# Pairing lone output tiles across sequences, and spreading a row by transposition

## The chip, the cores and the metric

The kernel runs on one core of a Trainium2 chip. The metric is the device time of one execution in microseconds (us), and the time before is the median of three runs. A profile of one execution goes with it. Engines are named as in the profile: PE is TensorE (PEld its weight loads), DVE is VectorE, ACT is ScalarE, POOL is GpSimd, SP is SyncE, which here issues almost all DMA.

## The reference

Attention with RMS-normalised q and k over 8 sequences, 12 heads, 448 tokens and head size 64 is followed by an RMS norm over the 768 features and a gated feed-forward block without bias (768 to 1536 to 768), all in float32. Shortened:

```python
def rmsnorm(x, g):
    return x / np.sqrt(np.mean(x * x, axis=-1, keepdims=True) + 1e-06) * g

q_n, k_n = rmsnorm(q, g_q), rmsnorm(k, g_k)          # (8, 12, 448, 64)
attn = softmax(q_n @ k_n.T / 8)
x = (attn @ v).transpose(0, 2, 1, 3).reshape(3584, 768)

xn = rmsnorm(x, rms_g)
g = xn @ w_gate                                      # (3584, 1536)
out = (g * sigmoid(g) * (xn @ w_val)) @ w_out        # (3584, 768)
```

## The kernel before

All eight sequences are worked off in one program. The attention of sequence b+1 is interleaved on TensorE with the feed-forward work of the sequences before it: a list of items is handed out between the attention steps in proportion to what the items cost. Items are the output products of sequence b-1 and then the gate and value products of sequence b. After the last sequence's attention the rest of the list runs alone.

**Strassen's scheme (Winograd's form).** From sequence 1 on, the gate and value products, and the output products, take 7 block products where a plain matrix product of 2x2 blocks takes 8. For the output product the left matrix is h (1536 features, kept with the features in partitions), its two block rows are two tiles of 128 tokens, "a pair", and its block columns are features 0 to 767 and 768 to 1535. The right matrix is w_out, cut into B11, B12, B21, B22 of 768 x 384 and the derived T1 to T4. Sequence 0 multiplies plainly with the unchanged blocks, since the derived ones are made only after all weights have been converted.

**Tiles of tokens.** 448 tokens are three and a half tiles. An even sequence leaves its last 64 tokens to the odd one after it, which then has 512, four tiles:

```python
for fc in (fp, fp + NFP):                            # NFP = 6: chunk of 128 features
    st["h", b, fc] = free_h.pop(0)
    if b % 2:
        before = st.pop(("h", b - 1, fc))
        nc.gpsimd.tensor_copy(st["h", b, fc][:, 0:64], before[:, S - 64:S])
        free_h.append(before)
```

So an odd sequence has two pairs; an even one from 2 on has one pair and a tile alone ("s"), which takes the four original blocks:

```python
def out_order(b):
    if b % 2:
        return [(name, (0, 1)) for name in ORDER_O]
    order = [(name, (0, "s") if name[0] == "B" else (0,)) for name in ORDER_O]
    return order[:-1] + [("B12", ("s",))] + order[-1:]

ORDER_O = ("B11", "B21", "T2", "T3", "T1", "B22", "T4")
```

The sums of the left blocks are made by VectorE in the same chunk's gate and value step (`quad`), four instructions of 128 x 128 for a pair and chunk:

```python
for pair in range(1 + b % 2) if b >= FIRST_O else ():            # FIRST_O = 1
    if fp == 0:
        st["so", b, pair] = {name: raw_pool.tile([128, NFP, 128], F32, name="so", tag="raw")
                             for name in ("S1", "S2", "S4")}
    of = lambda name: left_o(b, pair, name, fp)
    nc.vector.tensor_tensor(of("S1"), of("A21"), of("A22"), ALU.add)
    ...                                                          # cut: S2, S3, S4 alike
```

The products themselves: six matmuls for one name and one pair, in two halves of three. B21 adds onto the PSUM bank of B11, and B22 onto that of T1:

```python
def step(name, which, half, last):
    onto = {"B21": "B11", "B22": "T1"}.get(name)
    ...                                                          # cut: the bank of "s"
    first = onto is None
    if half == 0:
        bank[name, which] = fresh() if first else bank[onto, which]
    for c in range(3 * half, 3 * half + 3):
        ...                                                      # cut: a is the left block
        nc.tensor.matmul(ps, lhsT=a, rhs=data(("wo", b, name, c)), start=first and c == 0, ...)   # L1086
    ...
# done(name, pair), after the second half:
#   B11: ScalarE copies the bank to p1            B21: ScalarE copies the bank out as y
#   T2:  VectorE  u2 = bank + p1                  T3:  VectorE  u3 = bank + u2
#   T1:  VectorE  y = bank + u3                   B22: VectorE  y = bank + u2
#   T4:  VectorE  y = bank + u3
```

Sequence 0 multiplies each tile plainly, 12 matmuls for each half of 384 output columns (`project_out`, L983), for `tiles = 3 + b % 2` = 3 tiles.

**Weights.** They are converted once, in 72 pieces that go through load, ScalarE, VectorE and a GpSimd add (`convert`, one piece at a turn), and written to a scratch tensor in DRAM. After that a weight block of 128 x 384 is loaded anew for each use into one of a set of buffers. When the conversion is over, its own buffers join them:

```python
if turn_of["n"] == TURNS:
    free_w.extend(cv_pool.tile([128, BW], F32, name="top") for _ in range(4))   # 25 + 4
```

The derived blocks of sequence 1 and on (T1 to T4) are made by VectorE while sequence 1 is worked on, and written to the scratch tensor too.

**The row of the norm.** The factor of each token is made with tokens in partitions (rs, 112 x 4) and is needed as a row over tokens, the same in all 128 partitions. A matmul with the identity does it, rs being read with step 0 as a 112 x 128 weight:

```python
for t in range(NT):                                              # NT = 4, P = 112
    nc.tensor.matmul(ps[:, t * P:(t + 1) * P], lhsT=rs[:, t:t + 1].to_broadcast([P, 128]),
                     rhs=ident[0:P, 0:P], start=True, stop=True)                 # L649
```

VectorE then multiplies x by that row out of PSUM.

Of the kernel before, what the change touches and what calls it, by code (L numbers as in the profile page):

```python
# [20 lines left out]
NT, P = 4, 112  # L21
# [314 lines left out]
def safe_scores(  # L336
# [306 lines left out]
    def norm_x(b):  # L643
# [4 lines left out]
        for t in range(NT):  # L648
            nc.tensor.matmul(ps[:, t * P:(t + 1) * P], lhsT=rs[:, t:t + 1].to_broadcast([P, 128]), rhs=ident[0:P, 0:P],  # L649
                             start=True, stop=True)  # L650
# [101 lines left out]
    turn_of = {"n": 0}  # L752
    TURNS = len(pieces) + 7
# [9 lines left out]
    def convert():  # L763
# [18 lines left out]
        if turn_of["n"] == TURNS:  # L782

            free_w.extend(cv_pool.tile([128, BW], F32, name="top") for _ in range(4))
# [3 lines left out]
    def out_order(b):  # L788


        if b % 2:
            return [(name, (0, 1)) for name in ORDER_O]
        order = [(name, (0, "s") if name[0] == "B" else (0,)) for name in ORDER_O]
        return order[:-1] + [("B12", ("s",))] + order[-1:]
# [4 lines left out]
    for b in range(1, B):  # L799
# [4 lines left out]
        if b < FIRST_O:  # L804
            uses += [("wo", b, *block_of(n, fc)) for n in range(2) for fc in range(NFC)]
        else:
            uses += [("wo", b, name, c) for name, _ in out_order(b) for c in range(NFP)]
# [85 lines left out]
    def quad(b, fp):  # L893
# [33 lines left out]
        def p2():  # L927
            product(b, fp, "A12", "B21", onto=bank["a"])
            for fc in (fp, fp + NFP):
                st["h", b, fc] = free_h.pop(0)  # L930
                if b % 2:

                    before = st.pop(("h", b - 1, fc))
                    nc.gpsimd.tensor_copy(st["h", b, fc][:, 0:64], before[:, S - 64:S])
                    free_h.append(before)
# [21 lines left out]
        def sums():  # L957

            for pair in range(1 + b % 2) if b >= FIRST_O else ():
                if fp == 0:  # L960
                    st["so", b, pair] = {name: raw_pool.tile([128, NFP, 128], F32, name="so", tag="raw") for name in ("S1", "S2", "S4")}
# [14 lines left out]
    def project_out(b, n, i, part, last):  # L976
# [5 lines left out]
        for fc in range(part * each, (part + 1) * each):  # L982
# [4 lines left out]
            if last and n == 1 and b % 2:  # L987
                free_h.append(st.pop(("h", b, fc)))
# [23 lines left out]
    def left_o(b, pair, name, c):  # L1012
# [4 lines left out]
        i = 2 * pair + row - 1  # L1017
        return st["h", b, c + (col - 1) * NFP][:, i * 128:(i + 1) * 128]
# [3 lines left out]
    def out_strassen(b):  # L1022
# [27 lines left out]
        def done(name, pair):  # L1050
# [4 lines left out]
            elif name == "B21":  # L1055
                final(ps, pair, 0, 2 * pair)
# [4 lines left out]
            elif name == "T1":  # L1061
                final(ps, pair, 1, 2 * pair + 1, "u3")
            elif name == "B22":
                final(ps, pair, 1, 2 * pair, "u2")
            else:
                final(ps, pair, 0, 2 * pair + 1, "u3")

        def step(name, which, half, last):
            onto = {"B21": "B11", "B22": "T1"}.get(name)
            if which == "s":  # L1070
                first = name in ("B11", "B22")
                if first and half == 0:
                    bank["s"] = fresh()
                ps = bank["s"]
            else:
                first = onto is None
                if half == 0:
                    bank[name, which] = fresh() if first else bank[onto, which]
                ps = bank[name, which]
            for c in range(3 * half, 3 * half + 3):  # L1080
                if which == "s":
                    fc = c + (int(name[1]) - 1) * NFP
                    a = st["h", b, fc][:, 256:384]
                else:
                    a = left_o(b, which, LEFT_O[name], c)
                nc.tensor.matmul(ps, lhsT=a, rhs=data(("wo", b, name, c)), start=first and c == 0, stop=c == NFP - 1,  # L1086
# [4 lines left out]
                if last and b % 2 and name in ("T3", "T4"):  # L1091
                    free_h.append(st.pop(("h", b, c + (name == "T4") * NFP)))
            if half == 0:
                return
            if which != "s":
                done(name, which)
            elif not first:
                final(ps, which, int(name[2]) - 1, 2)

        for name, whose in out_order(b):  # L1100
            for which in whose:
# [286 lines left out]
```

## Time and profile before

| what | before |
|---|---|
| time, median of 3 runs (lowest to highest) | 1614.12 us (1612.43 to 1615.44) |
| span of the profiled execution | 1612.2 us |
| HBM read, written | 235.93 MB, 39.32 MB |
| output matmuls of pairs and lone tiles (L1086), program | 534 |
| plain output matmuls of sequence 0 (L983), program | 72 |
| row-spreading matmuls (L649), program | 32 |
| loads of output weights (w<-kept_o), as listed | 289, 192.0 KB each, 3.0 us to landing |

A page of the profile has six parts: the busy time of each engine; the span in 40 slices with a digit for the tenths that an engine was busy in each; the DMA queues; the chain of work that ended last, followed back from the last instruction, by engine and by line; the costliest groups of instructions (line, engine, operation, output<-inputs, shapes, count | busy us, mean ns of one | idle time of the engine just before, and what ended it); and the DMA issues. The trace can also be asked for the groups with shapes kept apart, for who waited for whom, for a timeline, for the chain in order of time, and for the busy time of the engines within given stretches. Ends of matmuls are modelled, and a matmul's listed duration overlaps that of the next. Idle time of an engine that isn't the bottleneck costs nothing.

### The profile page before, as it was taken

To read this page: it belongs to the slowest core of one execution; us is meant where nothing else is said; L and a number is where in the kernel's file an instruction comes from. 1 tells how busy PE (TensorE), PEld (TensorE's weight loads), DVE (VectorE), ACT (ScalarE), POOL (GpSimd) and SP (SyncE) were. 2 spreads that over 40 slices of the span, in tenths; PEclk is the share of its full clock that TensorE was granted. 3 is DMA by queue.
4 is the path that set the end of the run, shared out by engine and by line. 5 is a ranking of instruction groups with operands and counts; after the bars stand their busy time and mean duration, and the time that the engine had idled before them with its cause. 6 is when DMAs were issued, how large, how long until landed. Compare 5 with 4: busy or idle time off the path is not lost.

```text
span 1612.2 us, 21593 instructions
## 1 busy us (share of the span) xinstructions
PE 1584.4 (98%) x7342; PEld 1123.7 (70%) x7342; DVE 859.9 (53%) x1495; ACT 472.3 (29%) x944; POOL 645.8 (40%) x667
## 2 busy tenths in 40 slices
PE   8999999999999999999999999999999999999998
PEld 4344445678865788568875788658786588959974
DVE  5989899278852455426562354524565235433531
ACT  6746564223221232223222222322332122101010
POOL 6867877434432354225533443344343223100000
PEclk9999999999999999999999999999999999999999
DMA  7648574567765555565544755476454454567651
GB/s 205 207 137 255 171 240 137 166 216 240 236 209 162 159 163 150 176 202 160 158 126 132 206 157 153 118 225 193 131 163 135 143 172 119 152 188 233 174 151 49
DMA packets 264586, 276.81 MB, mean 172 GB/s; under 512 B 79124, under 2 KB 261396, under 8 KB 264468
## 3 DMA queue, kind: packets, MB, share of 16 engines
q1 hardware_dynamic: 263540, 275.15, 57.3%
q8 instruction: 60, 0.98, 0.2%
q14 instruction: 58, 0.48, 0.1%
q10 hardware_dynamic: 800, 0.20, 0.1%
q0 software_dynamic: 128, 0.00, 0.0%
HBM read 235.93 MB, written 39.32 MB: 171 GB/s over the span
## 4 chain that ended last, share of the span: by engine, by line
PE 83%; DVE 4%; issue 0%; ACT 0%; DMA 0%; POOL 0%; DVEq 0%
PE ff L888 41%; PE ff L1086 22%; PE sc L537 6%; PE av L589 5%; PE ff L983 3%; PE sc L567 2%; PE den L602 2%; PE tr L519 1%; DVE top L736 1%; DVE top L737 1%; DVE rd L610 1%; PE ff L1117 0%; DVE top L735 0%; PE rb L649 0%; PE msx L637 0%
## 5 line engine op out<-in xcount | busy, mean ns | idle before, releaser
L888 PE MATMUL ff<-x,w 128*128 128x224 f32 x1740 | 354.2, 353 | 1.4 <-DVE u L900 1.4
L888 PEld LDWEIGHTS ff<-x,w 128*128 128x128 f32 x1740 | 326.5, 190 | 11.6 <-issue 4.6
L547 POOL TENSOR_TENSOR es<-e 128x448 f32<-128x448 f32 x82 | 91.3, 1134 | 528.6 <-ACT e L541 528.6
L888 PE MATMUL ff<-xs,w 128*128 128x224 f32 x1314 | 269.7, 353 | 5.4 <-DVE w L845 4.0
L888 PEld LDWEIGHTS ff<-xs,w 128*128 128x128 f32 x1314 | 246.1, 190 | 11.5 <-issue 9.9
L1086 PE MATMUL ff<-w,h 128*128 128x384 f32 x582 | 198.3, 487 | 0.0
L554 POOL TENSOR_TENSOR es<-es,e 64x448 f32<-64x448 f32 (+1 forms) x164 | 190.8, 1174 | 6.3
L610 DVE RECIPROCAL rd<-rd 128x448 f32<-128x448 f32 x41 | 121.0, 2952 | 124.8 <-ACT rd L609 124.8
L541 ACT ACTIVATE e<-sc,rs 128x448 f32<-128x448 f32 x288 | 161.9, 635 | 49.6 <-PE sc L537 46.7
L1086 PEld LDWEIGHTS ff<-w,h 128*128 128x128 f32 x582 | 109.1, 190 | 75.1 <-issue 2.0
L537 PE MATMUL sc<-qT,kT 64*128 64x448 f32 x576 | 139.1, 575 | 3.5 <-ACT sq L478 2.0
L589 PE MATMUL av<-e,vt 128*64 128x448 f32 x576 | 118.8, 548 | 0.0
L1086 PE MATMUL ff<-w,so 128*128 128x384 f32 x338 | 116.1, 488 | 1.3 <-DVE y L1047 1.3
L498 POOL TENSOR_TENSOR rs<-ms,mhalf 128x12 f32<-128x12 f32 (+1 forms) x50 | 114.5, 2290 | 4.2
L537 PEld LDWEIGHTS sc<-qT,kT 64*128 64x128 f32 x576 | 54.7, 186 | 85.6 <-issue 69.2
L1117 PE MATMUL ff<-x,w 128*128 128x448 f32 x288 | 111.8, 541 | 0.0
L900 DVE TENSOR_TENSOR cc<-ff,u 128x448 f32<-128x448 f32 x84 | 52.4, 623 | 90.4 <-PE ff L888 90.2
L1086 PEld LDWEIGHTS ff<-w,so 128*128 128x128 f32 x338 | 63.1, 190 | 45.6 <-DVE y L1047 2.5
L773 POOL TENSOR_TENSOR w<-top,raw 128x384 int32<-128x384 int32 x72 | 77.5, 1090 | 38.0 <-DVE top L737 25.4
L589 PEld LDWEIGHTS av<-e,vt 128*64 128x64 f32 x576 | 37.1, 136 | 75.6 <-issue 75.6
L1117 PEld LDWEIGHTS ff<-x,w 128*128 128x128 f32 x288 | 53.3, 190 | 50.8 <-issue 49.0
L623 POOL TENSOR_TENSOR ss<-ss,rd 128x448 f32<-128x448 f32 x40 | 46.6, 1165 | 79.3 <-ACT rd L622 79.3
(125 smaller groups left out, 1900.2 us busy)
## 6 DMA issues: line engine op xcount, KB each, us to landing
w<-kept SPq DMA_DIRECT2D x475, 192.0 KB, 2.8
w<-kept_o SPq DMA_DIRECT2D x289, 192.0 KB, 3.0
kept<-w SPq DMA_DIRECT2D x91, 192.0 KB, 3.9
top<-kept SPq DMA_DIRECT2D x77, 192.0 KB, 3.6
qk<-in_q_dram SPq DMA_DIRECT2D x48, 192.0 KB, 3.1
qk<-in_k_dram SPq DMA_DIRECT2D x96, 96.0 KB, 3.6
vt<-in_v_dram SPq DMA_DIRECT2D x48, 192.0 KB, 2.5
raw<-in_moe_w_gate_dram SPq DMA_DIRECT2D x24, 384.0 KB, 4.5
```

The source lines that it names most:

```text
L498: nc.gpsimd.tensor_tensor(st["rs", g][:, cols], ms, mhalf[:, cols], ALU.pow)
L537: nc.tensor.matmul(ps[:, 0:S], lhsT=kT[r, c * 128:(c + 1) * 128], rhs=qT[r, :], start=True, stop=True)
L541: nc.scalar.activation(e, ps[:, 0:S], ACT.Exp, scale=rs[:, n:n + 1])
L547: nc.gpsimd.tensor_tensor(es, st["e", g, 0, j], st["e", g, 1, j], ALU.add)
L554: nc.gpsimd.tensor_tensor(es[r], es[r], e[r], ALU.add)
L589: nc.tensor.matmul(av[own(j), 0:S], lhsT=vt[:, j, c], rhs=st["e", g, c, j], start=False, stop=(c == NK - 1), skip_group_check=True)
L610: nc.vector.reciprocal(rd, rd)
L773: nc.gpsimd.tensor_tensor(data(key).bitcast(I32), top, lo, ALU.add)
L888: nc.tensor.matmul(bank[:, w * HT:(w + 1) * HT], lhsT=wt[:, c * 128:(c + 1) * 128], rhs=x[:, c, :], start=onto is None and w == c == 0, st ...
L900: nc.vector.tensor_tensor(add[name], ps[:, 0:S], add[other], ALU.add)
L1086: nc.tensor.matmul(ps, lhsT=a, rhs=data(("wo", b, name, c)), start=first and c == 0, stop=c == NFP - 1, skip_group_check=True)
L1117: nc.tensor.matmul(bank[w][:, 0:S], lhsT=data(key)[:, c * 128:(c + 1) * 128], rhs=st["x", 0, half][:, c, :], start=half == c == 0, stop=ha ...
```

## The change

It has two parts.

The tiles of four sequences are now arranged together. A tile without a partner is not multiplied alone; its columns of h are copied by GpSimd into 12 "carried" tiles (128 x 128 each, index -1 below) and become the first tile of the next sequence's first pair. Sequence 0 multiplies two tiles plainly and carries its third, sequence 1 has four tiles and the carried one and carries its last, sequence 2 has three and the carried one, and sequence 3 takes sequence 2's last 64 tokens and has four; then it begins anew, with one pair in sequence 4. It is meant to save matmuls, as a tile in a pair takes fewer of them.

Room is made for it: the carried tiles and the sums S1, S2, S4 live in the former buffers of the conversion, so two buffers instead of four join the weight buffers. The blocks of h of a sequence that carries are given back later, after the copies.

The second part makes the row of the norm by TensorE's transposition instead of a matmul with the identity. The values are the same.

```diff
@@ norm_x
-            nc.tensor.matmul(ps[:, t * P:(t + 1) * P], lhsT=rs[:, t:t + 1].to_broadcast([P, 128]), rhs=ident[0:P, 0:P],
-                             start=True, stop=True)
+            nc.tensor.transpose(ps[:, t * P:(t + 1) * P], rs[:, t:t + 1].to_broadcast([P, 128]), ident[0:P, 0:P])
@@ convert
-            free_w.extend(cv_pool.tile([128, BW], F32, name="top") for _ in range(4))
+            free_w.extend(cv_pool.tile([128, BW], F32, name="top") for _ in range(2))
+            whole = [raw_pool.tile([128, 2 * BW], F32, name="raw") for _ in range(7)]
+            room_so.extend(whole[:6])
+            homes = [whole[6][:, 0:BW], whole[6][:, BW:]] + [cv_pool.tile([128, BW], F32, name="top") for _ in range(2)]
+            carried.extend(t[:, i * 128:(i + 1) * 128] for t in homes for i in range(3))
@@ in place of out_order
+    def out_pairs(b):
+        return (((0, 1),), ((-1, 0), (1, 2)), ((-1, 0), (1, 2)), ((0, 1), (2, 3)))[b % 4]
+
+    def carries(b):
+        return b % 4 < 2
@@ quad, p2
-                if b % 2:
+                if ("h", b - 1, fc) in st:
                     before = st.pop(("h", b - 1, fc))
-                    nc.gpsimd.tensor_copy(st["h", b, fc][:, 0:64], before[:, S - 64:S])
+                    if b % 2:
+                        nc.gpsimd.tensor_copy(st["h", b, fc][:, 0:64], before[:, S - 64:S])
+                    if carries(b - 1):
+                        at = out_pairs(b - 1)[-1][1] + 1
+                        nc.gpsimd.tensor_copy(carried[fc], before[:, at * 128:(at + 1) * 128])
                     free_h.append(before)
@@ quad, sums
-            for pair in range(1 + b % 2) if b >= FIRST_O else ():
+            for pair in range(len(out_pairs(b))):
                 if fp == 0:
-                    st["so", b, pair] = {name: raw_pool.tile([128, NFP, 128], F32, name="so", tag="raw") for name in ("S1", "S2", "S4")}
+                    st["so", b, pair] = {name: room_so[3 * pair + i].rearrange("p (c n) -> p c n", c=NFP)
+                                         for i, name in enumerate(("S1", "S2", "S4"))}
@@ left_o
-        i = 2 * pair + row - 1
-        return st["h", b, c + (col - 1) * NFP][:, i * 128:(i + 1) * 128]
+        i, fc = out_pairs(b)[pair][row - 1], c + (col - 1) * NFP
+        return carried[fc] if i < 0 else st["h", b, fc][:, i * 128:(i + 1) * 128]
@@ step: the branches for "s" go; the order is now
-        for name, whose in out_order(b):
-            for which in whose:
+        pairs = out_pairs(b)
+        for name in ORDER_O:
+            for which in range(len(pairs)):
                 for half in range(2):
@@ out_items, sequence 0
-        tiles = 3 + b % 2
+        tiles = out_pairs(b)[-1][1] + 1
```

Cut: the list of weight uses, which follows the same order, and the places where blocks of h are given back.

## The prediction

> **What bounds the kernel now.** I read the page first: the share of each engine, then the 40 slices, then the chain that ended last. The kernel runs on one core.
>
> ```profile
> span 1612.2 us, 21593 instructions
> PE 1584.4 (98%) x7342; PEld 1123.7 (70%) x7342; DVE 859.9 (53%) x1495; ACT 472.3 (29%) x944; POOL 645.8 (40%) x667
> PE   8999999999999999999999999999999999999998
> ...
> PEclk9999999999999999999999999999999999999999
> ...
> PE 83%; DVE 4%; issue 0%; ACT 0%; DMA 0%; POOL 0%; DVEq 0%
> PE ff L888 41%; PE ff L1086 22%; PE sc L537 6%; PE av L589 5%; PE ff L983 3%; PE sc L567 2%; PE den L602 2%; PE tr L519 1%; DVE top L736 1%; DVE top L737 1%; DVE rd L610 1%; PE ff L1117 0%; DVE top L735 0%; PE rb L649 0%; PE msx L637 0%
> ```
>
> TensorE (PE) is busy 98% of the span at full clock in every slice, and it holds 83% of the chain. All that is idle on it is 1612.2 - 1584.4 = 27.8 us. So the change is worth, first of all, what it takes off TensorE, and after that what it does to those few waits. L888 (gate and value products) is not touched; L1086 (paired output products), L983 (plain output products of sequence 0) and L649 (the row spread) are.
>
> Next I took the groups of TensorE with shapes kept apart, for how many records one matmul leaves, and the timeline for what one really takes. The durations in a group overlap one another (a matmul's end includes its drain), so I take the distance between starts.
>
> ```profile
> L1086 PE MATMUL ff<-w,h 128*128 128x384 f32 x582 | 198.3, 487 | 0.0
> ...
> L983 PE MATMUL ff<-w,h 128*128 128x384 f32 x144 | 47.7, 488 | 0.0
> ...
> L519 PE MATMUL tr<-ident,qn 128*128 128x128 f32 x144 | 24.0, 275 | 1.6 <-POOL qn L503 1.4 <-DMA kept<-w 0.2
> ...
> L649 PE MATMUL rb<-ident,rs 112*128 112x112 f32 x64 | 8.4, 275 | 1.0 <-POOL rs L641 1.0
> ```
>
> Counting the program: L983 issues 3 tiles x 2 halves x 12 = 72 matmuls and leaves 144 records; L649 issues 8 x 4 = 32 and leaves 64. A float32 matmul leaves two records. L519's transposes of q are 48 x 3 = 144 and leave 144: a transpose leaves one.
>
> ```profile
> 439.61 0.49 PE L519 MATMUL tr<-ident,qn 128*128 128x128 f32 x3
> 439.94 0.27 PE L523 MATMUL tr<-ident,rest 128*128 128x128 f32 x1
> ...
> 450.21 1.04 PE L649 MATMUL rb<-ident,rs 112*128 112x112 f32 x8
> 451.09 2.12 PE L1086 MATMUL ff<-w,h 128*128 128x384 f32 x6
> ```
>
> Columns: start, length, engine, line. Three transposes of 128 columns take 439.94 - 439.61 = 0.33 us, 0.11 us each. The four spreading matmuls take 451.09 - 450.21 = 0.88 us, 0.22 us each. For an output matmul I take the chain of waits in order of time, whose last long piece is the output of the last sequence, without attention between:
>
> ```profile
> 1551.41 54.19 PE ff L1086 x168
> ```
>
> 168 records are 84 matmuls: 54.19 / 84 = 0.645 us each.
>
> Last, who waited for whom on TensorE:
>
> ```profile
> PE ff L888 <- DVE w L845: 4.0, 2, 2.5
> PE ff L888 <- DVE u L900: 2.8, 2, 1.4
> PE ff L1086 <- DVE y L1047: 2.0, 3, 0.7
> ```
>
> The first two all lie between 316 and 448 us: the gate and value products of sequence 1, whose weight differences are made by VectorE (DVE) while it is also the busiest there (102 of 132 us). The third is the product of an unpaired even sequence: B22 adds onto T1's PSUM bank, and with one pair TensorE comes to it at once and has to wait until VectorE has read T1. Three even sequences (2, 4, 6), three waits.
>
> **What the Trainium skill says.** "Perfetto Trace Analysis", section Transposes, asks that logical transposes use the transpose operation and not a standard matmul, since it has a path that skips arithmetic. The trace agrees: one record in place of two, 0.11 us against 0.22 us. The same page, section Tensor Engine Instruction, says that a matmul's end in the profile is an estimate; here starts are 0.645 us apart for two records that are listed at 487 ns each, which is why I use starts. Its section Matmuls wants accumulation groups to rotate through banks so that evacuation overlaps; the three L1086 waits of 0.65 us are where that rotation is missing. "SBUF — State Buffer", in its summary rules, says that a VectorE instruction with two SBUF inputs contends with a GpSimd instruction that reads SBUF; the added copies and sums are of these kinds. No wait in the lists names it, so I give it only a place in the range.
>
> **The change part by part.**
>
> 1. Fewer output matmuls. A tile alone costs 24 (12 contraction chunks x 2 halves); a pair costs 7 products x 6 = 42, so 21 a tile. 3584 tokens are 28 tiles. Before: sequence 0 has 3 plain tiles, sequences 2, 4, 6 have one alone each, the other 22 make 11 pairs: 6 x 24 + 11 x 42 = 606. After: sequence 0 keeps 2 plain tiles (its weights are then still blocks of the original matrix), its third goes to sequence 1, and so on; the pairs by sequence are 2, 2, 2, 1, 2, 2, 2 = 13: 48 + 546 = 594. Twelve fewer: 12 x 0.645 = 7.7 us off TensorE, all on the path.
>
> 2. The row spread as a transpose. 32 instructions at 0.11 in place of 0.22 us (112 columns instead of 128 make it a shade less): 4 x 8 x 0.11 = 3.6 us off TensorE, on the path too, as it stands in TensorE's order between products that don't wait.
>
> 3. Waits of the accumulation onto a bank. Sequences 2 and 6 get two pairs, so another pair's product lies between; their waits of 0.65 us go. Sequence 4 now has one pair and nothing between: B21 follows B11 onto its bank directly, so it must wait until ScalarE has copied B11 out (479 ns in the groups, about 0.6 us with signalling). T1 to B22 keeps its wait, but a turn of four transposes (0.44 us) falls between in the changed order, which leaves some 0.2 us. From 2.0 to 0.9 us: 1.1 us won.
>
> 4. What is added elsewhere. VectorE: two more pairs of sums, 2 x 6 x 4 = 48 instructions of 128x128 at about 0.35 us (the four groups in before have 335 to 381 ns), 17 us. Evacuations: four lone tiles lose 8, two pairs gain 14. GpSimd: 48 copies of 128x128 into the carried tiles; the 128x64 copy takes 319 ns, so I estimate under 0.5 us each, 24 us at most. VectorE at 53% and GpSimd at 40% have room in sequences 2, 5 and 6. All are off the path except in sequence 1 (below).
>
> 5. Buffers. Two weight buffers go to the carried tiles, so 27 remain. In a full sequence a weight is asked for some 42 us of TensorE work ahead instead of 45 (program order, with the durations above); landing takes 3 us. In sequence 4, where one pair uses up a block every 0.65 us, the smallest lead is some 18 us. Weight loads also fall by 18, as lone tiles needed B12 too. I count nothing.
>
> 6. The step from sequence 0 to 1. With 24 of its 72 plain matmuls gone (the pairs get them back later), the products of sequence 1 begin 24 x 0.645 = 15.5 us earlier, while the conversion of the last weights doesn't come earlier. GpSimd's last conversion ends at 286.9 us in before. By the changed order, I work out that TensorE wants it at about 284 us, but it now stands ahead of the smaller-half sums of the softmax on GpSimd, so it should be ready at about 283 us. The reload of weights then follows at some 284 to 288 us, VectorE's differences at 288 to 291, and TensorE wants the first of them at about 301 us. That is close, but it holds: 0 to 1.5 us lost.
>
> Sum: 7.7 + 3.6 + 1.1 - 0.5 (point 6) = 11.9 us. 1614.1 - 11.9 = 1602.2 us.
>
> **The rivals.**
>
> A: the wait of sequence 1 grows. It has 6.8 us of waits on VectorE, which gets 12 GpSimd copies as neighbours and less lead from the plain products. For it: VectorE is at 9.8 of 10 us in 340 to 350, 370 to 380 and 410 to 420 us, just where TensorE drops to 8.2 to 8.6. Against it: the number of sums is unchanged in sequence 1, and that stage also gets more attention work between its products, as the work is spread by cost over the same slots. If it doubled, some 6 us would be given back: 1608.
>
> B: the conversion of the output weights becomes the bound at 275 to 290 us, since TensorE gets there earlier than VectorE and GpSimd. For it: VectorE is full there (9.3 to 9.8 of 10 us until 280). Against it: the order above, and only the last two of 72 blocks are close. It would give 2 to 4 us back: 1605.
>
> C: weights come late with 27 buffers. For it: 228 GB/s over sequence 1. Against it: leads of 18 to 42 us against 3. It would show as TensorE waiting on DMA: 1606 or more. I hold it for unlikely.
>
> D: shifted order breaks up the remaining waits in sequence 1, so that 2 to 4 us are won on top: 1599.
>
> **Range and chances.** The counted part (11.3 us) is firm to about 1 us; A to D pull by -3 to +6, and three runs of before spread over 3 us. So 1602 with 1598 to 1607. Two per cent is 32 us; for faster the change would have to remove more than all the idle time of TensorE, for slower three times the waits would have to come on top. Faster 0.01, same 0.97, slower 0.02.
>
> **What would show it.** Output records go from 1068 + 144 to 1092 + 96 (24 fewer), the spread's from 64 to 32 with four of them in 0.4 to 0.45 us: point 1 and 2. L1086's waits on VectorE fall, and a wait on ScalarE's p1 copy appears once, in sequence 4: point 3. TensorE's busy time falls by some 11 us, to about 1573. Idle time of TensorE stays within 24 to 31 us; if it grows, the list of waits names the rival: w or u from VectorE in sequence 1 is A, GpSimd's converted w ahead of the plain product is B, DMA is C. I am wrong if TensorE's busy time falls by other than 10 to 13 us, or if a wait of more than 4 us appears that before doesn't have.

## The result, and the profile after

| | before | after |
|---|---|---|
| time, median (lowest to highest) | 1613.28 us (1612.23 to 1615.44, four runs) | 1602.96 us (1602.87 to 1604.57, four runs) |
| span of the profiled execution | 1612.2 us | 1601.2 us |
| TensorE busy, idle in that span | 1584.4, 27.8 us | 1574.3, 26.9 us |

The ratio of the times is 0.9937 (95% interval 0.9919 to 0.9954): 10.3 us won, where 11.9 were predicted.

The page of the changed kernel: the span, the busy time of each engine, and the shares of the chain that ended last.

```profile
span 1601.2 us, 21577 instructions
PE 1574.3 (98%) x7286; PEld 1115.9 (70%) x7286; DVE 879.0 (55%) x1553; ACT 469.9 (29%) x940; POOL 658.7 (41%) x715
...
PE 81%; DVE 5%; POOL 0%; issue 0%; DMA 0%; ACT 0%; SPq 0%; DVEq 0%; POOLq 0%
```

TensorE is still the bound, and nearly all of the gain is work that it no longer has. VectorE and GpSimd took on 19 and 13 us, and the span shows little of it. The groups of TensorE in the changed kernel (shapes kept apart; count, then busy us and mean ns, then the idle time before) tell what went. Line numbers move with the edit: L989 is the plain product of sequence 0, L1079 the paired product, L649 the row spread, L889 the gate and value product.

```profile
L1079 PE MATMUL ff<-w,h 128*128 128x384 f32 x498 | 167.8, 487 | 0.6 <-ACT p L1058 0.6
L1079 PE MATMUL ff<-w,raw 128*128 128x384 f32 x468 | 159.5, 487 | 0.3 <-DVE y L1051 0.3
L989 PE MATMUL ff<-w,h 128*128 128x384 f32 x96 | 32.3, 490 | 0.1
...
L649 PE MATMUL rb<-ident,rs 112*128 112x112 f32 x32 | 4.4, 260 | 1.0 <-POOL rs L641 1.0
```

With four smaller groups of the same line (48, 44, 30 and 4 records) L1079 has 1092 records, and L989 has 96. At two records a matmul that is 594 matmuls in place of 606. The spread has one record an instruction now. How long the four of them take is seen in the timeline of TensorE in the changed kernel, as the distance between starts:

```profile
250.53 0.55 PE L649 MATMUL rb<-ident,rs 112*128 112x112 f32 x4
250.92 7.92 PE L989 MATMUL ff<-w,h 128*128 128x384 f32 x24
```

That is 0.39 us, where the kernel before took 0.88.

Who waited for whom on TensorE in the changed kernel (us in total, times, longest):

```profile
PE ff L889 <- DVE w L846: 3.3, 3, 1.5
PE ff L889 <- DVE h L912: 2.6, 3, 1.0
PE ff L889 <- DVE u L901: 1.9, 1, 1.9
...
PE ff L1079 <- ACT p L1058: 0.6, 1, 0.6
...
PE ff L1079 <- DVE y L1051: 0.3, 1, 0.3
```

The three waits for T1's bank (2.0 us) are gone, and sequence 4 has the 0.6 and 0.3 us in their place that were predicted. The waits of sequence 1 fell from 6.8 to 5.2 us. The second line is new: three waits of 0.7 to 1.0 us on `h`, which no part of the prediction has.

Where these lie is seen by cutting the span at the eight row spreads, which stand at the same place of each sequence's work. The table has the times between their starts, and what the count of matmuls and the predicted saving at the spread would have made of them; waits are not in that column. H ends with the last output matmul.

| stretch (what lies in it) | before | after | difference | by the count |
|---|---|---|---|---|
| start to the first spread | 97.67 | 96.04 | -1.63 | 0 |
| A: gate and value of sequence 0 | 155.08 | 154.49 | -0.59 | -0.45 |
| B: output 0, gate and value 1 | 197.46 | 181.98 | -15.48 | -15.93 |
| C: output 1, gate and value 2 | 197.33 | 197.93 | +0.60 | -0.45 |
| D: output 2, gate and value 3 | 186.63 | 197.82 | +11.19 | +11.16 |
| E: output 3, gate and value 4 | 197.32 | 196.83 | -0.49 | -0.45 |
| F: output 4, gate and value 5 | 186.63 | 171.17 | -15.47 | -15.93 |
| G: output 5, gate and value 6 | 193.34 | 194.07 | +0.74 | -0.45 |
| H: output 6, gate and value 7, output 7 | 193.64 | 203.78 | +10.14 | +11.16 |

The agreement in D is luck: the wait of 0.65 us for T1's bank that went and a new wait of 0.72 us cancel there.

The new waits are in C, D and G: 0.83, 0.72 and 1.02 us. The first of them, in TensorE's timeline of the changed kernel (in brackets the idle time before, and who ended it):

```profile
558.40 1.30 PE L889 MATMUL ff<-xs,top 128*128 128x224 f32 x6
559.53 1.30 PE L889 MATMUL ff<-xs,w 128*128 128x224 f32 x6
561.66 2.54 PE L889 MATMUL ff<-x,w 128*128 128x224 f32 x12 [0.83 <-DVE h L912]
```

And VectorE up to that moment:

```profile
555.64 1.44 DVE L912 SCALAR_TENSOR_TENSOR h<-h,cc 128x448 f32<-128x448 f32 x1
557.12 1.11 DVE L969 TENSOR_TENSOR raw<-h,h 128x128 f32<-128x128 f32 x1
558.33 1.09 DVE L970 TENSOR_TENSOR raw<-raw 128x128 f32<-128x128 f32 x1
559.35 0.28 DVE L971 TENSOR_TENSOR h<-raw,h 128x128 f32<-128x128 f32 x1
...
560.48 0.28 DVE L972 TENSOR_TENSOR raw<-h,raw 128x128 f32<-128x128 f32 x1
...
560.81 0.38 DVE L911 SCALAR_TENSOR_TENSOR h<-th,ff 128x224 f32<-128x224 f32 x1
561.22 0.39 DVE L912 SCALAR_TENSOR_TENSOR h<-h,ff 128x224 f32<-128x224 f32 x1
```

L911 and L912 read the bank of the chunk's first product (`ff`), and the product that waits, A22 with T4, gets its bank only when they have ended. Ahead of them stand eight sums now (L969 to L972, two pairs), where the kernel before had four at this place. Two of the eight take 1.1 us instead of 0.28. GpSimd, at the same time:

```profile
553.51 0.29 POOL L939 COPY raw<-h 128x128 f32<-128x128 f32 x1
553.74 0.29 POOL L939 COPY top<-h 128x128 f32<-128x128 f32 x1
554.00 5.28 POOL L554 TENSOR_TENSOR es<-es,e 128x448 f32<-128x448 f32 x4
```

The slow sums are those that lie beside L554, which ends at 559.28; the sums after it take 0.28 us. This is the contention that the Trainium skill, "SBUF — State Buffer", section Who interferes with whom, states for a VectorE instruction with two SBUF inputs beside a GpSimd instruction that reads SBUF. The prediction kept a place for it in the range only. The two copies of the change (0.29 us each) push L554 back by some 0.5 us.

More sums or slow sums alone don't make the wait. In the kernel before, at this place in stretch C, two of the four sums were slow as well:

```profile
574.88 1.11 DVE L963 TENSOR_TENSOR so<-h,h 128x128 f32<-128x128 f32 x1
576.03 1.17 DVE L964 TENSOR_TENSOR so<-so,h 128x128 f32<-128x128 f32 x1
...
578.06 0.39 DVE L911 SCALAR_TENSOR_TENSOR h<-h,ff 128x224 f32<-128x224 f32 x1
```

They ended in time: the product with T4 began at 578.86 without a wait. In stretch G of the changed kernel another chunk has eight sums of 0.28 to 0.29 us each, from 1358.74 on, and no wait either. And in stretch D both kernels have eight sums, as sequence 3 has two pairs in both, and no tile is carried out of sequence 2. New at that place is only that two of the eight lie beside L554 and take 1.1 us each.

### The profile page after: what moved, and what is told of

The parts are those of the page before. It is cut to its first block, busy times and chain, and to the rows that moved or that the text cites. A ratio compares the mean times of both kernels' runs of the same rounds, so it can differ in the third digit from the quotient of the medians.

```text
span 1601.2 us, 21577 instructions
## 1 busy us (share of the span) xinstructions
PE 1574.3 (98%) x7286; PEld 1115.9 (70%) x7286; DVE 879.0 (55%) x1553; ACT 469.9 (29%) x940; POOL 658.7 (41%) x715
## 4 chain that ended last, share of the span: by engine, by line
PE 81%; DVE 5%; POOL 0%; issue 0%; DMA 0%; ACT 0%; SPq 0%; DVEq 0%; POOLq 0%
PE ff L889 40%; PE ff L1079 22%; PE sc L537 6%; PE av L589 5%; PE sc L567 2%; PE den L602 2%; PE tr L519 1%; PE ff L989 1%; DVE top L735 1%; DVE top L736 1%; DVE top L734 0%; PE ff L1107 0%; DVE rd L610 0%; DVE h L912 0%; DVE h L911 0%
## 5 line engine op out<-in xcount | busy, mean ns | idle before, releaser
L889 PE MATMUL ff<-x,w 128*128 128x224 f32 x1878 | 383.2, 355 | 4.4 <-DVE h L912 2.6
L889 PEld LDWEIGHTS ff<-x,w 128*128 128x128 f32 x1878 | 352.5, 191 | 20.2 <-issue 11.1
L889 PE MATMUL ff<-xs,w 128*128 128x224 f32 x1374 | 281.7, 353 | 3.3 <-DVE w L846 3.3
L889 PEld LDWEIGHTS ff<-xs,w 128*128 128x128 f32 x1374 | 258.1, 190 | 7.1 <-issue 6.0
L554 POOL TENSOR_TENSOR es<-es,e 64x448 f32<-64x448 f32 (+1 forms) x164 | 191.8, 1180 | 6.3
L1079 PE MATMUL ff<-w,h 128*128 128x384 f32 x498 | 167.8, 487 | 0.6 <-ACT p L1058 0.6
L1079 PE MATMUL ff<-w,raw 128*128 128x384 f32 x468 | 159.5, 487 | 0.3 <-DVE y L1051 0.3
L1079 PEld LDWEIGHTS ff<-w,h 128*128 128x128 f32 x498 | 93.5, 190 | 64.5 <-issue 1.3
L1079 PEld LDWEIGHTS ff<-w,raw 128*128 128x128 f32 x468 | 87.6, 190 | 60.9 <-issue 2.6
L1107 PEld LDWEIGHTS ff<-x,w 128*128 128x128 f32 x288 | 53.3, 190 | 50.8 <-issue 49.0
```

The source lines that it names most:

```text
L554: nc.gpsimd.tensor_tensor(es[r], es[r], e[r], ALU.add)
L889: nc.tensor.matmul(bank[:, w * HT:(w + 1) * HT], lhsT=wt[:, c * 128:(c + 1) * 128], rhs=x[:, c, :], start=onto is None and w == c == 0, st ...
L1079: nc.tensor.matmul(ps, lhsT=left_o(b, which, LEFT_O[name], c), rhs=data(("wo", b, name, c)), start=first and c == 0, stop=c == NFP - 1, sk ...
L1107: nc.tensor.matmul(bank[w][:, 0:S], lhsT=data(key)[:, c * 128:(c + 1) * 128], rhs=st["x", 0, half][:, c, :], start=half == c == 0, stop=ha ...
```

## The experiments

**Theory.** The gain is the count of matmuls and the spread; what is missing of it are the new waits, and they come from the sums' place in VectorE's queue. **Rivals:** the contention with GpSimd makes the waits, wherever the sums stand; the carried copies on GpSimd make them; sequence 1's weights and buffers take the rest.

### The spread alone

```diff
 # the kernel before, with one line changed in norm_x
-            nc.tensor.matmul(ps[...], lhsT=rs[...].to_broadcast([P, 128]), rhs=ident[0:P, 0:P], start=True, stop=True)
+            nc.tensor.transpose(ps[...], rs[...].to_broadcast([P, 128]), ident[0:P, 0:P])
```

> The kernel before with the transposition alone. The sum of the prediction: the eight row spreads take 0.43 instead of 0.88 us each and nothing else moves, so 3.6 us less than before, 1609.7 us, ratio 0.9978. Rival 1: the spread lies beside other work and TensorE only waits elsewhere for the time won, ratio 1.000. Rival 2: the spread also brings VectorE's scaling of x forward and takes waits away in sequence 1, over 5 us, ratio under 0.997. The distances between the starts of the spreads should be those of before less 0.45 us each, but for windows at half clock (1.7 us each).

Measured: 1610.58 us beside 1614.13 us before in the same series, ratio 0.9981 (0.9974 to 0.9988). Each of the stretches C to H is 0.49 or 0.50 us shorter than before, so eight spreads give 3.9 us. B is 1.06 us longer in its profile, as TensorE was granted half its clock for some microseconds in it (1.7 us of clock are missing between 408 and 414 us); the last section shows such stretches. The waits of sequence 1 and those on T1's bank are the same as before. So this part does what was counted, and only that.

### The pairs alone

```diff
 # the changed kernel, with one line put back in norm_x
-            nc.tensor.transpose(ps[...], rs[...].to_broadcast([P, 128]), ident[0:P, 0:P])
+            nc.tensor.matmul(ps[...], lhsT=rs[...].to_broadcast([P, 128]), rhs=ident[0:P, 0:P], start=True, stop=True)
```

> The changed kernel with the matmul for the row spread put back. The ledger of the two traces: 12 fewer output matmuls (-7.7), waits of the bank of T1 and B11 (-1.1), new waits for VectorE behind the second pair's sums (+2.5): 6.3 us less than before and 3.6 us more than the changed kernel: 1607 us, ratio 0.996. Rival: without new waits, or with the parts helping each other, it would be 9 us less (ratio 0.9944), or the whole gain of the changed kernel would not be the sum of the parts.

Measured: 1607.05 us, ratio 0.9955 (0.9942 to 0.9969). Stretches C to H are those of the changed kernel plus 0.5 us each, and the waits are the same three, 3.3, 2.6 and 1.9 us. The two parts (3.55 and 7.08 us in the medians) add up to 10.6 us, and together they brought 10.3. They don't disturb each other, and all the new waits belong to the pairs.

### The sums two products later

`after(n, f)` puts f off until n more items have been handed out. The sums were put off by three items, which is just ahead of the two instructions that free the bank.

```diff
         def p3_last():
             p3()
-            after(3, sums)
+            after(5, sums)
```

> The changed kernel with the sums S1 to S4 handed to VectorE two steps later. Theory: the new waits of 0.8, 0.7 and 1.0 us of gate and value products on VectorE's h arise since eight sums instead of four stand ahead of the two instructions that free the PSUM bank of the first product; with the sums behind them these three waits go, 2.5 us less than the changed kernel, 1600.5 us, and the wait of sequence 1 on u3 (1.9 us) may go too. Rival: the waits come from contention of GpSimd with VectorE, whatever stands in the queue; then they stay or move, and the time is that of the changed kernel, 1603.

Measured: 1599.84 us, ratio 0.9912 (0.9897 to 0.9927): 3.1 us better than the changed kernel by the medians, and 2.5 us by stretches C to G of the profiles. VectorE in this kernel, in the same place:

```profile
556.11 0.38 DVE L911 SCALAR_TENSOR_TENSOR h<-th,ff 128x224 f32<-128x224 f32 x1
556.52 0.39 DVE L912 SCALAR_TENSOR_TENSOR h<-h,ff 128x224 f32<-128x224 f32 x1
...
558.28 0.28 DVE L969 TENSOR_TENSOR raw<-h,h 128x128 f32<-128x128 f32 x1
...
560.02 0.28 DVE L972 TENSOR_TENSOR raw<-h,raw 128x128 f32<-128x128 f32 x1
```

Counted from the spread at which the stretch begins (432.51 us in the changed kernel, 430.80 here), L911 starts 3.0 us earlier. The eight sums follow, and they cost TensorE nothing there. All that TensorE waits for on its feed-forward banks from 430 to 1400 us in this kernel is:

```profile
PE ff L1079 <- ACT p L1058: 0.6, 1, 0.6
PE ff L1079 <- DVE y L1051: 0.3, 1, 0.3
PE ff L889 <- DVE u L901: 0.3, 1, 0.3
```

Stretches C, D and E are 196.83 us each, and G is 192.78, as the count has it. C, D and G are 1.11, 0.99 and 1.29 us shorter than in the changed kernel, so by the stretches the waits cost 3.4 us, more than the 2.6 listed. With the same sums and copies, their place in the queue decides whether TensorE waits. Contention by itself does not: L911 and L912 of the second half of the chunk before are still slow beside L554 here (1.39 and 1.46 us). But the sums have also left the neighbourhood of L554, so the run doesn't tell what their slowness alone was worth. By the timeline it is 1.65 us in C, more than the wait of 0.83 us; so, as an estimate, sums of 0.28 us each at the old place would not have made TensorE wait. No run here tries that. On the other side stands F, 0.85 us longer than in the changed kernel; the third wait of the list lies there and accounts for 0.3 of it.

### The carried copies on ScalarE

```diff
-                        nc.gpsimd.tensor_copy(carried[fc], before[:, at * 128:(at + 1) * 128])
+                        nc.scalar.copy(carried[fc], before[:, at * 128:(at + 1) * 128])
```

> The changed kernel with the 48 copies into the carried tiles on ScalarE instead of GpSimd. Theory: these copies don't cause the new waits on VectorE's h (they last 0.3 us each; it is the number of sums ahead and the long softmax sums on GpSimd), so the waits of 0.8, 0.7 and 1.0 us stay within 0.3 us and the time is that of the changed kernel, 1603 us. Rival: the copies hold up VectorE, and the waits fall by more than half, 1601 or less.

Measured: 1602.3 us, ratio 0.9928 (0.9915 to 0.9942). Of 2.6 us of waits on `h`, 1.5 remain: C is 0.46 us shorter, G 0.59, D as it was. Neither side had the size. So the copies add about 1 us; how they do it isn't shown, as in C the same two sums are slow without them (1.11 and 1.16 us). D, where none are made, is unchanged. The waits that remain show that the copies aren't the cause by themselves.

### Sequence 4 in another order

Sequence 4 has a single pair, so B21 follows B11 onto its bank. This kernel gives a sequence with one pair an order of products of its own, in which others lie between; `ORDER` is the order that the gate and value products use.

```diff
+    def names_of(b):
+        return ORDER_O if len(out_pairs(b)) == 2 else ORDER
-        uses += [("wo", b, name, c) for name in ORDER_O for c in range(NFP)]
+        uses += [("wo", b, name, c) for name in names_of(b) for c in range(NFP)]
-        for name in ORDER_O:
+        for name in names_of(b):
```

> The changed kernel with sequence 4, the only one with one pair, in the order B11, T2, B21, T3, T1, T4, B22, so that another product lies between the two that share a bank. Theory: the waits of 0.6 us (on ScalarE's copy of B11) and 0.3 us (on VectorE's reading of T1) go: 0.9 us less than the changed kernel, 1602.1 us. Rival: the time is set by another bank (three in all), and a wait of the same length appears on T1 or T4: 1603.

Measured: 1601.91 us, ratio 0.9926 (0.9912 to 0.9939). Stretch F falls from 171.17 to 169.74 us, and no wait on a bank is left in it. The 0.6 and 0.3 us were real; the other 0.5 us isn't explained. The remaining stretches are as in the changed kernel, but for B, 1.6 us shorter with the same waits. That is taken up in the last section.

### Both

The two edits together (sums later, order for one pair).

> The changed kernel with the sums two steps later and the lone pair in the order B11, T2, B21, T3, T1, T4, B22. If the two parts add up: 2.5 to 3.1 us for the sums and 0.9 to 1.4 us for the order, so 1599 us, ratio to before 0.9906. If the sums of sequence 4 now meet the new order, a wait of TensorE on VectorE of 0.5 to 1 us appears in sequence 4 and half of the order's gain is gone.

Measured: 1598.21 us, ratio 0.9904 (0.9889 to 0.9919). C, D and E are 196.83 us, G 192.78, F 170.59: the gain of each edit is kept, less 0.85 us in F, where the later sums cost what they did alone.

### Fewer buffers

The question is whether the two buffers that the change takes cost anything. First four fewer than the change leaves, then two; then the kernel before gets two fewer.

```diff
-    NW, NH = 25, 14
+    NW, NH = 21, 14      # changed kernel: 23 buffers in all after the conversion (27 with 25)
```

> The changed kernel with four more weight buffers taken away, 23 in place of 27 after the conversion (the change itself took two). Theory: weights are asked for 42 us of TensorE work ahead and land in 3, with 23 buffers still 37 us ahead, so nothing changes outside of sequence 1; in sequence 1, where the differences need buffers too, less than 2 us: 1603 to 1605. Rival: buffers were the price of the change (0.3 us or more for each), then 1604 to 1606, with TensorE waiting on DMA in sequences 2 to 7.

Measured: 1613.59 us, ratio 1.0003 (0.9994 to 1.0011). All of the gain is gone. The loss lies in one stretch: B is 191.61 us, 9.6 more; C to H are within 0.05 us of the changed kernel. A is 0.55 us longer, and the time ahead of the first spread 1.7 us, with a stretch of half clock in it. TensorE waits in it on weight differences for 10.9 us, where it was 3.3. One of these waits, from TensorE's timeline of this kernel:

```profile
426.63 4.85 PE L889 MATMUL ff<-xs,w 128*128 128x224 f32 x12 [5.47 <-DVE w L846]
```

and VectorE's timeline ahead of it:

```profile
424.02 6.76 DVE L846 TENSOR_TENSOR w<-w,w 128x384 f32<-128x384 f32 x6
```

Six differences of weights stand in a clump, 1.1 us each, and the product that needs them comes at once. With few buffers a difference can't be made ahead, since it needs a buffer for its result; it is made at the last moment, on the path. And the eight sums of the chunk before stand ahead of the clump, from 421.22 to 424.02 us: 2.8 of the 5.5 us of this wait are theirs. I had expected transfers to come late and under 2 us. It is VectorE's order, and about five times that.

```diff
-    NW, NH = 25, 14
+    NW, NH = 23, 14      # changed kernel: 25 buffers
```

> The changed kernel with two more weight buffers taken away, 25 in place of 27. With 23 the stretch of sequence 1's products took 191.6 us instead of 182.0 and all other stretches were as before. If the loss is a threshold (the differences of weights no longer come in time only below some number), 25 keeps the stretch at 182 to 184 us and the time at 1603 to 1605; if each buffer has its price, it lies half-way, 187 us and 1608.

Measured: 1600.69 us, ratio 0.9919 (0.9902 to 0.9935). With 25 buffers stretch B is 179.24 us, shorter than with 27, and by 1.1 us still when the half clock in B of the changed kernel (last section) is left out. Neither branch had this.

```diff
-    NW, NH = 25, 14
+    NW, NH = 23, 14      # kernel before: 27 buffers, as the changed kernel has
```

> The kernel before with two buffers fewer, 27 in place of 29: that part of the change alone. Point 5 of the prediction counts nothing for it: 1613.5 us, ratio within 0.0015 of 1, the stretch of sequence 1 at 197.5 us. Rival: the two buffers cost in sequence 1 as the four did in the changed kernel; then 2 to 5 us more, with the waits of gate and value products on weight differences above 7 us.

Measured: 1628.55 us, ratio 1.0092 (1.0075 to 1.0109). Here the two buffers cost 15 us, again all in stretch B (212.53 us). Who waited for whom in this kernel, first line, and one of its waits in TensorE's timeline:

```profile
PE ff L888 <- DVE w L845: 15.5, 4, 5.3
```

```profile
371.71 2.61 PE L888 MATMUL ff<-xs,w 128*128 128x224 f32 x6 [5.27 <-DVE w L845]
```

VectorE during that wait:

```profile
366.51 0.28 DVE L963 TENSOR_TENSOR so<-h,h 128x128 f32<-128x128 f32 x1
...
368.85 1.21 DVE L965 TENSOR_TENSOR h<-h 128x128 f32<-128x128 f32 x1
369.98 1.21 DVE L966 TENSOR_TENSOR so<-h,so 128x128 f32<-128x128 f32 x1
371.12 0.55 DVE L845 TENSOR_TENSOR w<-w,top 128x384 f32<-128x384 f32 x1
```

For 4.6 of the 5.27 us VectorE works on eight sums, three of them slow (1.1 to 1.2 us), and only the rest is the late difference. The other wait of 5.27 us, which ends at 446.86, is made in the same way. So these waits, too, are those of work that stands behind the sums in the queue. Waits account for 8.7 of the 15 us (15.5 for 6.8); most of the rest is half clock behind them (last section).

I counted in the instruction order of each kernel how many of the 48 weight differences stand directly ahead of the products that need them:

| kernel | buffers | made at the last moment | stretch B, us |
|---|---|---|---|
| before | 29 | 17 | 197.46 |
| before | 27 | 36 | 212.53 |
| changed | 27 | 15 | 181.98 |
| changed | 25 | 24 | 179.24 |
| changed | 23 | 40 | 191.61 |

36 and 40 go with waits of over 5 us; 15 to 24 don't order the times. So it isn't the number of buffers that costs, but the order that comes out of it and what then stands ahead of the late differences, and that order doesn't follow the number evenly. Why two buffers fewer double the late differences in the kernel before, and why 25 beat 27 in the changed one, I could not settle. More than 27 in the changed kernel weren't tried.

### The best version

To the two edits, one copy of k's transpose is moved from VectorE to ScalarE for sequence 2 only, whose attention shares stretch B with sequence 1's products; then the same with 25 and with 26 buffers.

```diff
-            nc.vector.tensor_copy(st["kT", g][:, FULL], ps[:, FULL])
+            if b == 2:
+                nc.scalar.copy(st["kT", g][:, FULL], ps[:, FULL])
+            else:
+                nc.vector.tensor_copy(st["kT", g][:, FULL], ps[:, FULL])
```

> The kernel of the two better orders, with the copy of k's transposes out of PSUM (0.55 us, one for each pair of heads) on ScalarE instead of VectorE while sequence 1's gate and value products run. Theory: what is left of waits there (3.3 us on weight differences, 1.6 us on another sum) comes from VectorE's queue, so six copies fewer, 3.3 us of its time, take 1 to 2 us of the waits: 1597 to 1598 us. Rival: the waits come from VectorE being held up by GpSimd's softmax sums at that moment; then less than 0.5 us, and scores may wait for ScalarE.

> The kernel of the two better orders and the copy on ScalarE, with 25 instead of 27 weight buffers. In the changed kernel 25 buffers took 2.7 us off the stretch of sequence 1 (1.7 of it a window at half clock that was missing). If the weights' order is the cause and independent of the rest, the stretch falls by 1 us or so from 179.8 us, to 178.8, and the time is 1596 us. If the gain with 25 was only a coincidence of that one order, the stretch is 180 to 184 us and the time 1597 to 1601.

> The same with 26 buffers. If fewer buffers help by themselves, it lies between, 1596.5 us; if the order of the differences within sequence 1 decides, it can lie anywhere between 1596 and 1602, and the list of waits for weight differences goes with it.

Measured: 1596.98 us with 27 buffers (ratio 0.9897, 0.9882 to 0.9913), 1597.46 us with 25 (0.9904, 0.9888 to 0.9921), 1596.78 us with 26 (0.9897, 0.9880 to 0.9914). The three can't be told apart by their medians. The copy gives 0.4 us in stretch B (180.13 to 179.76), and the waits there are as they were (3.3 us on differences, 1.7 on another sum), so the 1 to 2 us of the theory did not come. The two profiles with and without it differ otherwise ahead of the first spread, by 1.8 us, which is not its doing. With 25 buffers B is 179.13 us, near the 178.8 of the first branch, and with 26 it is 178.61 us, shorter than with either 25 or 27; the waits on differences are 3.3 us in all three, so they don't explain it. All are faster than the changed kernel by 5.5 to 6.2 us, over half of what the change itself brought, on top of it.

## Why the prediction was right, and where it was not

The predicted time was 1602 us (1598 to 1607) and the measured one is 1602.96. By its points:

1. **Fewer output matmuls: right.** 594 of them, and stretches B, D, F and H move by -15.48, +11.19, -15.47 and +10.14 us, where -15.93 and +11.16 were counted without waits. With the lost wait of 0.65 us the count for D and H is 10.5, and D without its new wait (sums two products later) moves by 10.20.

2. **The spread: right, a little undersized.** 0.49 us a spread instead of 0.45, so 3.9 us instead of 3.6; the spread alone shows it.

3. **Waits of a bank: right.** The 2.0 us are gone, and 0.9 us stand in sequence 4, as said.

4. **"All are off the path except in sequence 1": this is the step that failed.** It rested on shares: VectorE at 53% and GpSimd at 40% have room in sequences 2, 5 and 6. They had. But the two instructions that free a bank stand behind eight sums in VectorE's queue, and where two of the eight lie beside GpSimd's additions and take 1.1 us instead of 0.28, TensorE waits, however idle VectorE is afterwards. That cost 2.6 us as listed, 3.4 us by the stretches, in the products of sequences 2, 3 and 6. In 2 and 6 four of the eight are new; in 3 none are, only the meeting with GpSimd is. So the contention that the prediction kept in the range alone belonged in the sum. Moving the sums behind these instructions removed these waits, at a price of 0.85 us in one stretch; moving the copies off GpSimd took away some 1 us of them.

5. **"Buffers. I count nothing": right in its outcome, and not for its reason.** I judged leads of transfers. Outside sequence 1 that holds: with four buffers fewer still, stretches C to H keep their times. In sequence 1 it is the differences made by VectorE that need buffers ahead of time, and there the same two buffers cost the kernel before 15 us when they were taken from it alone. The changed order happened to come out well: that is luck.

6. **The step to sequence 1: right.** 0.3 us were lost where 0 to 1.5 were allowed and 0.5 counted. TensorE and GpSimd in the changed kernel there:

```profile
279.27 8.25 PE L989 MATMUL ff<-w,h 128*128 128x384 f32 x24
287.44 0.59 PE L567 MATMUL sc<-qT,kT 64*64 64x448 f32 x2
...
296.85 2.43 PE L889 MATMUL ff<-x,w 128*128 128x224 f32 x12
```

```profile
279.41 1.98 POOL L773 TENSOR_TENSOR w<-top,raw 128x384 int32<-128x384 int32 x2
```

The 24 matmul records from 279.27 on took 8.17 us from start to start, where the same number took 7.85 at 250.92. The conversion ended at 281.4 us, 1.6 earlier than estimated, and TensorE came to the first product that takes a difference at 299.12, some 2 us earlier than estimated.

**The rivals.** A (the waits of sequence 1 grow) is refuted by the list of waits: 6.8 to 5.2 us. D (they shrink by 2 to 4 us) had the direction and not the size. B didn't occur beyond the 0.3 us. C (weights late by transfer) has no wait on a DMA to show for it. TensorE's idle time, 26.9 us, stayed in the range of 24 to 31, and its busy time fell by 10.1 us, at the lower edge of 10 to 13.

**The sum.** The two profiles are 11.0 us apart, and each holds one stretch of half clock before its last output (1.7 us; last section), ahead of the first spread in the kernel before and in B in the changed one; these cancel. Missed were terms of opposite sign: +2.6 to 3.4 us of new waits, and -1.6 us of waits in sequence 1. With the spread's 0.3 us and 0.2 us at the step to sequence 1 they make 0.5 to 1.3 us, and 0.9 us are missing between the predicted gain of 11.9 and these 11.0. The medians' 10.3 also hold how many such stretches each run happened to have. So the closeness of the total owes something to cancelling terms, but the two large ones, 11.3 us of the 11.9, were measured one by one.

## What to carry to other kernels

Added work on an engine with room is free only if nothing that another engine waits for stands behind it in that engine's queue: for each place where work is added, look up which instruction frees the next bank, and put the new work after it. Count the work at the time it takes beside its neighbours, which was four times its time alone for some of the sums here. A buffer count is judged not only by how early transfers land, but by whether anything is computed into these buffers ahead of its use; there a smaller number changes the order of the instructions, and the effect can be zero or fifteen microseconds. Cutting two traces at a recurring instruction and setting each stretch against its count of matmuls finds waits of under a microsecond that the shares of the page hide.

## What the hardware showed that I had not expected

**Stretches of half clock, 3.4 us long, without a long pause before them.** Stretch B of the changed kernel is 1.6 us longer than in the kernel with another order for sequence 4, although both have the same waits there. TensorE in the changed kernel, then in the other:

```profile
390.14 2.72 PE L889 MATMUL ff<-xs,w 128*128 128x224 f32 x12 [1.46 <-DVE w L846]
...
401.85 4.22 PE L889 MATMUL ff<-x,w 128*128 128x224 f32 x12 [1.85 <-DVE u L901]
```

```profile
402.20 2.54 PE L892 MATMUL ff<-x,w 128*128 128x224 f32 x12 [1.86 <-DVE u L904]
```

Twelve records take 4.05 us from start to start (the next instruction starts at 405.90) against 2.37 us. The stretch from 400 to 407 us in the two kernels (busy time and instruction count of PE, PEld, DVE, ACT and POOL, then the granted clock, DMA share and GB/s):

```profile
400.00:407.00 7.00, 5.15 (x19) 4.82 (x19) 5.26 (x11) 0.17 (x1) 2.00 (x6) 0.76 0.92 288
```

```profile
400.00:407.00 7.00, 5.14 (x30) 4.52 (x30) 6.70 (x14) 0.39 (x1) 2.35 (x6) 1.00 0.91 269
```

A granted clock of 0.76 over 7 us is half clock for 3.4 us, which costs 1.7 us of work; in cuts of 0.5 us the clock is 0.50 from 402.5 to 405.5 and 1.00 before and after. The kernel before has such a stretch too, at 11.8 us (0.83 over 10 us, where the changed kernel has 1.00), and that is the -1.63 us of the first row of the table. The prediction read "full clock in every slice" from the page's digits; a 9 there means 90% or more, and 1.7 us of a slice of 40 us don't show. The Trainium skill, "TensorE: Matmul & The Clock Gate", Part 1, states half clock after an idle window of about 3.4 us, with windows that run freely. The length agrees; the pause does not, as here two pauses of 1.46 and 1.85 us, 12 us apart, were enough in one run and not in another with the same pauses. Which run gets one is chance as far as these traces show.

It also explains, as an inference, why the runs of one kernel lie in steps: before has runs near 1612.7, 1614.3 and 1615.7 us, the changed kernel near 1602.9 and 1604.6. With none, one or two such stretches a run is 0, 1.6 or 3.2 us longer. The mean clocks recorded with these runs of the kernel before go along: 0.998 or 0.999 at the lowest step, 0.997 or 0.998 at the middle one, 0.997 at the highest. Differences of under 2 us between kernels here are therefore read from the stretches of the trace, and not from medians.

**Long waits bring more of it.** In the kernel before with 27 buffers, two cuts around waits of 5.3 us:

```profile
368.00:378.00 10.00, 6.29 (x22) 5.89 (x23) 8.50 (x10) 0.00 (x0) 5.89 (x5) 0.66 0.38 124
442.00:456.00 14.00, 9.14 (x39) 8.69 (x40) 10.48 (x17) 2.45 (x6) 6.33 (x5) 0.76 0.47 146
```

3.4 and 3.4 us of clock are missing there (10 x 0.34, 14 x 0.24), half clock for 6.8 us each. In cuts of 1 us it begins 2.8 to 2.9 us after TensorE fell idle, so 2.4 us of it pass in the wait itself, and the other 4.4 us cost 2.2 us of work. So a wait of 5 us on a late difference cost nearly half as much again. A third stretch, of 1.7 us of work, follows a wait of 2.47 us at 416.5 us. With the 8.7 us of waits these three make 14.8 of the 15.07 us that stretch B lost.
